# Four query halves of a clustered-attention block keep their softmax in float32, and every step is put into a new order

## The chip, the core and the metric

The kernel runs on one core of a Trainium2 chip. The core has five engines that work side by side and wait for one another by semaphores: TensorE (PE in the profile; its weight loads are the row PEld), VectorE (DVE), ScalarE (ACT), GpSimd (POOL) and SyncE (SP), which issues the DMAs. Each engine works through its own instructions in the order in which the program lists them. The metric is the time of one run in device microseconds.

## The reference

Three blocks follow one another. First comes attention over 16 heads (2 batches of 8 heads, 768 tokens, 64 wide), in which a query sees only those keys that fall to the same one of 16 centroids:

```python
q_assign = argmax(q_n @ c_n.T);  k_assign = argmax(k_n @ c_n.T)
mask   = q_assign[:, None] == k_assign[None, :]
scores = where(mask, 0.125 * q @ k.T, -1e9)
attn   = exp(scores - max(scores)); attn /= sum(attn) + 1e-9
out    = attn @ v                                   # per head: 768 x 768 @ 768 x 64
```

Its output is reshaped to 1536 tokens of 512 and goes through two dense blocks in float32:

```python
h = x @ w_in;   x = elu(h) @ w_out                  # 512 -> 2048 -> 512
y = ((x @ w_a) * (x @ w_b)) @ w_out2                # 512 -> 1536 -> 512
```

## The kernel before

**Tiles.** The 16 heads `g` are worked in 8 pairs `j` (heads 2j and 2j+1). A head's 768 queries are 6 tiles `t` of 128 rows, and three tiles make a half `f`: 0 for t = 0, 1, 2 and 1 for t = 3, 4, 5. So there are 96 query tiles and 16 halves of pairs. Every step is a small function marked `@op`, and the string `ORDER` at the top lists some 2280 steps (`sc:3.1` is the score step of head 3, tile 1). The program runs through that list once, so the list sets the order on every engine, and each step may also name the buffer that it takes (`/sc=0`). No planner is in the program; the list is all there is.

**One query tile.** `sc` (line 692) makes a 128 x 768 tile of scores on PE: four float32r matmuls of 384 columns, since query and key are split into parts that restore the precision, and the cluster mask is a part of the same product. `rm` (L700) finds the row maximum on DVE, into `nm`. `ex` (L713) takes the exponential on ACT, from the scores in PSUM to `pf`, float32 in SBUF, with the row sums beside it. Then the probabilities must be transposed, and this is done in one of two ways.

- *Over PE:* `tr` (L746) transposes half a tile (three 128 x 128 blocks) to PSUM in `tt`; `th` (L750) copies that to float16 on ACT or DVE, the high part; `tl` (L755) subtracts on DVE what `th` has stored from `tt` and writes the rest, the low part, in float16 too.
- *Over DMA:* `hi` (L721) writes a float16 copy of `pf` into `phl`, on ACT or POOL; `lo` (L728) writes the rest there, on POOL or DVE; `td` (L760) has a DMA transpose both into the same place.

In both cases `pt` then holds the transposed probabilities of a half as two float16 parts.

**The product with v.** `av` (L805) makes the product of a half for both heads of a pair, in three pieces (n = 0, 1, 2). V is split as well, into float16 parts `v1` and `v2` (L519, L524), and three of the four combinations are formed: 6 key blocks x 3 combinations x 2 heads = 36 matmuls of 384 columns. The two heads write to the upper and lower 64 partitions of one PSUM tile. `ra`, `rc`, `rx`, `rb` and `re` bring 1 / sum into the layout of that tile (sum + 1e-9 on ACT, reciprocal on DVE, spread on POOL, a transpose on PE, a copy from PSUM), and `ev` (L815) multiplies and stores it into `acc`, over the place in which this pair's V was staged.

**Operands.** `lq`, `lk` and `lp` load a head's queries and a pair's keys, `ka1`, `ka2`, `qa` (L582 on ACT, L584 on POOL), `qb` (L507, DVE), `kb`, `kbd` split them, and `sm`, `m1` to `m5`, `oh`, `ohs`, `ohd` work out the cluster of every query and key of a pair (`sm`, L604, is 12 float32 matmuls of up to 128 columns). `wl`, `wa`, `w0` to `w4`, `wh`, `ws`, `wq` load the float64 weights as integers and make two float32r parts of them on ACT, DVE and POOL. `wm` (L432) is eight bf16 matmuls on zeros that fill PE's idle time at the start. `vr` (L454) looks for the largest V on ACT.

**The dense blocks** `h`, `x2`, `ab`, `o` (L944 to L946) are three float32r matmuls for each product. They begin when the first tokens are through attention.

Of the kernel before, what the change touches and what calls it, by code (L numbers as in the profile page):

```python
# [71 lines left out]
lq:2.0/rawq=0 wm:19 vr:6 tr:0.1.0/tt=2 vr:7 vr:8 wm:22 vr:9 vr:10 vr:11 sc:0.2/sc=0 th:0.1.1.0/pt=0
lq:3.0/rawq=1 tl:0.1.1 vr:12 ka1:2.2 ka1:3.2 vr:13 vr:14 vr:15 th:0.1.0.0 ka2:2.2 lp:1.0/rawp=1 wh:0
mo:0 wm:25 wl:1 rm:0.2/nm=2 sb:0 ws:0 sc:1.0/sc=1 wm:33 wm:34 wm:35 lk:2.0/rawk=0 wq:0 th:0.0.0.0
rm:1.0/nm=3 tl:0.1.0 ex:0.2/pf=2 vtp:0/tt=1 wm:36 wm:37 sc:1.1/sc=0 vtd:0 tl:0.0.0 vbp:0/tt=2 wm:38
hi:0.2.1/phl=0 vbd:0 vs:2 ex:1.0/pf=1 rm:1.1/nm=0 wa:1 tr:1.0.0/tt=1 tr:1.0.1/tt=0 qa:2.1
ex:1.1/pf=1 sc:1.2/sc=1 qa:3.1 w0:1 sm:1/tt=2 lo:0.2.0 sc:0.3/sc=0 wm:39 wm:40 hi:1.1.1/phl=1 w1:1
qb:2.0 w2:1 td:0.2 rm:1.2/nm=1 rm:0.3/nm=2 lo:1.1.2 vs:3 th:1.0.1.1/pt=1 m1:1/mx=1 tl:1.0.1
th:1.0.0.1 vs:0 m2:1 ex:1.2/pf=2 sc:0.5/sc=1 rm:0.5/nm=3 ex:0.3/pf=1/sum=1 hi:1.2.1/phl=2 wh:1 vs:1
tl:1.0.0 sc:0.4/sc=0 rm:0.4/nm=0 tr:0.0.1/tt=0 wm:41 wm:42 wm:43 v1:0.1/v1=0 v1:2.1/v1=1 td:1.1  # L80
lp:2.0/rawp=0 th:0.0.1.1 lo:1.2.2 ex:0.5/pf=0 kbd:2 w3:1 sc:1.3/sc=1 hi:0.5.1/phl=3 qb:3.0 w4:1 m3:1
tr:0.3.1/tt=1 wm:44 wm:45 wm:46 lq:4.0/rawq=0 ka1:4.1 lo:0.5.2 th:0.3.1.1/pt=2 ex:0.4/pf=2
v2:0.2/v2=0 rm:1.3/nm=1 m4:1 m5:1/oht=1 wl:2 tl:0.0.1 sc:1.5/sc=0 oh:1/tt=2 tl:0.3.1 v1:1.1/v1=2
tr:0.3.0/tt=0 ra:0.0/rs=0 v2:1.2/v2=1 td:1.2 tr:0.4.1/tt=1 ex:1.3/pf=0 ohs:1/ohs=0 sc:1.4/sc=1
rm:1.5/nm=2 ka2:3.2 th:0.3.0.1 tl:0.3.0 ex:1.5/pf=1 qa:4.1 rc:0.0 th:0.4.1.0 tr:1.3.1/tt=2
tr:0.4.0/tt=0 rm:1.4/nm=3 ohd:1 av:0.0.0 kbd:3 th:0.4.0.1 tl:0.4.1 av:0.0.1 th:1.3.1.1/pt=3
sc:2.0/sc=0 ex:1.4/pf=2 tl:0.4.0 tl:1.3.1 tr:1.3.0/tt=1 ws:1 rx:0.0/rx=0 sc:2.1/sc=1 wq:1
v1:3.1/v1=3 ka2:4.0 hi:1.5.1/phl=0 hi:1.4.1/phl=1 qb:4.0 ra:0.1/rs=1 av:0.0.2 rm:2.0/nm=0 ka1:5.1
th:1.3.0.1 ex:2.0/pf=0/sum=0 sc:2.2/sc=0 lp:6.0/rawp=1 td:0.5 tr:2.0.1/tt=0 rm:2.1/nm=1 lo:1.4.2
tl:1.3.0 kbd:5 wa:2 v2:3.2/v2=2 lo:1.5.0 ex:2.1/pf=2 rb:0.0/tt=2 sc:3.0/sc=1 th:2.0.1.1/pt=0  # L90
re:0.0.1/rb=0 tr:2.1.0/tt=1 lq:5.0/rawq=1 tr:2.1.1/tt=2 td:1.4 rm:2.2/nm=2 rc:0.1 tl:2.0.1 ka2:5.2
ex:2.2/pf=1 th:2.1.1.1 tr:2.0.0/tt=0 w0:2 sc:3.1/sc=0 hi:2.2.1/phl=2 rx:0.1/rx=1 rm:3.0/nm=3
rm:3.1/nm=0 kbd:4 tl:2.1.1 ex:3.0/pf=2 rb:0.1/tt=2 ev:0.0 v2:2.2/v2=3 qa:5.1 lk:3.0/rawk=1
ex:3.1/pf=0 lq:7.0/rawq=0 td:1.5 re:0.1.1/rb=1 sc:2.3/sc=1 hi:3.1.1/phl=3 lo:2.2.2 w1:2 qb:5.0
th:2.1.0.1 sc:3.2/sc=0 w2:2 lo:3.1.2 rm:3.2/nm=1 sm:2/tt=2 wh:2 rm:2.3/nm=2 w3:2 w4:2 lq:8.0/rawq=1
ex:3.2/pf=1 sc:2.4/sc=0 tl:2.1.0 tr:3.0.0/tt=1 ex:2.3/pf=0/sum=1 m1:2/mx=0 ws:2 hi:3.2.1/phl=1
rm:2.4/nm=3 th:2.0.0.1 m2:2 lo:3.2.2 wl:3 sc:2.5/sc=1 th:3.0.0.1/pt=1 av:0.1.0 tl:2.0.0 vs:11 m3:2
rm:2.5/nm=0 tr:3.0.1/tt=0 td:3.1 ka1:6.1 av:0.1.1 ex:2.4/pf=1 m4:2 m5:2/oht=0 th:3.0.1.1 sc:3.3/sc=0
wq:2 hi:2.4.1/phl=0 ex:2.5/pf=2 oh:2/tt=2 tl:3.0.1 wa:3 vs:4 td:2.2 ra:1.0/rs=0 ohs:2/ohs=1
sc:3.4/sc=1 lo:2.4.0 hi:2.5.2/phl=3 rm:3.3/nm=1 ex:3.3/pf=1 tr:2.3.0/tt=0 av:0.1.2 tr:2.3.1/tt=2  # L100
w0:3 td:3.2 th:2.3.0.1/pt=2 rm:3.4/nm=2 sc:3.5/sc=0 tl:3.0.0 tr:3.3.0/tt=1 ev:0.1 ohd:2 ka2:6.2
rc:1.0 av:1.0.0 ex:3.4/pf=0 lo:2.5.2 tl:2.3.0 qa:7.1 rm:3.5/nm=3 th:3.3.0.1/pt=3 rx:1.0/rx=0 ka1:7.1
ex:3.5/pf=2 av:1.0.1 tl:3.3.0 sc:4.0/sc=1 w1:3 hi:3.5.1/phl=2 tr:3.3.1/tt=0 ka2:7.0 qb:7.0
rm:4.0/nm=0 hi:3.4.1/phl=1 sc:4.1/sc=0 av:1.0.2 lo:3.5.2 rb:1.0/tt=1 th:3.3.1.1 vs:8 td:2.4
ra:1.1/rs=1 rc:1.1 td:2.5 rm:4.1/nm=1 ex:4.0/pf=1/sum=0 tl:3.3.1 sc:4.2/sc=1 th:2.3.1.1 vs:5
tr:4.0.0/tt=0 tl:2.3.1 rm:4.2/nm=2 tr:4.0.1/tt=2 th:4.0.0.0/pt=0 ex:4.1/pf=2 re:1.0.1/rb=0
th:4.0.1.1 lp:3.0/rawp=0 rx:1.1/rx=1 ex:4.2/pf=1 sc:5.0/sc=0 lo:3.4.2 rm:5.0/nm=3 tr:4.1.0/tt=1
v1:5.1/v1=0 hi:4.2.2/phl=0 lo:4.2.2 kbd:6 tl:4.0.0 ex:5.0/pf=0 sc:5.1/sc=1 lq:6.0/rawq=0 th:4.1.0.1
rb:1.1/tt=0 tl:4.0.1 rm:5.1/nm=0 v2:5.2/v2=0 re:1.1.1/rb=1 td:3.5 sc:5.2/sc=0 tr:5.0.0/tt=2 qa:6.1
tl:4.1.0 tr:5.0.1/tt=0 td:3.4 ex:5.1/pf=1 rm:5.2/nm=1 lk:4.0/rawk=0 w2:3 hi:5.1.1/phl=3 qb:6.0  # L110
th:5.0.1.1/pt=1 ex:5.2/pf=0 ev:1.0 tl:5.0.1 sm:3/tt=1 lo:5.1.2 sc:4.3/sc=1 sc:4.4/sc=0 m1:3/mx=1
v1:4.1/v1=2 rm:4.3/nm=2 ra:2.0/rs=0 tr:4.1.1/tt=0 m2:3 hi:5.2.1/phl=2 rm:4.4/nm=3 ex:4.3/pf=1/sum=1
th:4.1.1.1 m3:3 rc:2.0 av:1.1.0 ex:4.4/pf=2 m4:3 hi:4.4.1/phl=1 sc:4.5/sc=1 vs:7 rm:4.5/nm=0
m5:3/oht=1 av:1.1.1 qa:8.1 th:5.0.0.0 sc:5.3/sc=0 tl:4.1.1 lo:5.2.2 v2:4.2/v2=1 rx:2.0/rx=0
oh:3/tt=1 rm:5.3/nm=1 av:1.1.2 td:4.2 vs:6 ex:4.5/pf=0 lo:4.4.2 ohs:3/ohs=0 ev:1.1 ex:5.3/pf=2
sc:5.4/sc=1 tr:4.3.1/tt=0 tr:4.3.0/tt=1 ka1:8.2 sc:5.5/sc=0 lq:9.0/rawq=0 th:4.3.1.1/pt=2 tl:5.0.0
lk:5.0/rawk=1 v1:7.1/v1=1 ka2:8.2 td:5.1 rm:5.4/nm=2 tl:4.3.1 hi:4.5.1/phl=0 rm:5.5/nm=3 qa:9.2
td:5.2 tr:5.3.1/tt=2 lp:4.0/rawp=0 w3:3 av:2.0.0 tr:5.3.0/tt=0 ex:5.4/pf=1 av:2.0.1 ohd:3 td:4.4
hi:5.4.1/phl=3 th:5.3.0.1/pt=3 kbd:7 ex:5.5/pf=2 sc:6.0/sc=1 sc:6.1/sc=0 qb:8.0 ra:2.1/rs=1 qb:9.0
lo:5.4.2 tl:5.3.0 rm:6.0/nm=0 td:5.4 rb:2.0/tt=0 th:4.3.0.1 lo:4.5.2 av:2.0.2 tl:4.3.0 rm:6.1/nm=1  # L120
th:5.3.1.1 ex:6.0/pf=1/sum=0 rc:2.1 w4:3 sc:6.2/sc=1 kbd:8 vs:14 hi:5.5.1/phl=2 rm:6.2/nm=2
re:2.0.1/rb=0 ex:6.1/pf=0 tr:6.0.0/tt=1 tr:6.0.1/tt=0 ex:6.2/pf=1 tl:5.3.1 sc:7.0/sc=0
th:6.0.0.0/pt=0 tl:6.0.0 rm:7.0/nm=3 tr:6.1.1/tt=2 sc:7.1/sc=1 td:4.5 hi:6.2.1/phl=1 lo:5.5.2 ev:2.0
ka1:9.1 vs:12 th:6.1.1.1 th:6.0.1.1 sm:4/tt=1 rm:7.1/nm=0 tl:6.0.1 td:5.5 lo:6.2.2 rx:2.1/rx=1
tr:6.1.0/tt=0 ex:7.0/pf=2 ex:7.1/pf=1 v1:6.1/v1=3 tl:6.1.1 vs:9 m1:4/mx=0 td:6.2 sc:7.2/sc=0
th:6.1.0.0 rb:2.1/tt=2 hi:7.1.1/phl=3 rm:7.2/nm=1 m2:4 ka2:9.2 sc:6.3/sc=1 av:2.1.0 re:2.1.1/rb=1
ex:7.2/pf=0 tr:7.0.0/tt=2 tl:6.1.0 sc:6.4/sc=0 hi:7.2.1/phl=0 rm:6.3/nm=2 lo:7.1.2 v2:7.2/v2=2 m3:4
tr:7.0.1/tt=0 av:2.1.1 rm:6.4/nm=3 ra:3.0/rs=0 m4:4 ex:6.3/pf=1/sum=1 th:7.0.1.1/pt=1 v2:6.2/v2=3
sc:6.5/sc=1 rc:3.0 ex:6.4/pf=2 m5:4/oht=0 hi:6.4.1/phl=2 oh:4/tt=1 th:7.0.0.1 lo:7.2.2 tl:7.0.1
sc:7.3/sc=0 av:2.1.2 tr:6.3.1/tt=0 rm:6.5/nm=0 tl:7.0.0 ohs:4/ohs=1 ex:6.5/pf=0 rx:3.0/rx=0 wl:4  # L130
rm:7.3/nm=1 lq:10.0/rawq=1 lq:11.0/rawq=0 lo:6.4.2 ka1:10.2 ev:2.1 ex:7.3/pf=2 tr:6.3.0/tt=2
sc:7.5/sc=1 hi:6.5.1/phl=1 th:6.3.1.0/pt=2 ka2:10.2 td:7.1 qa:10.1 th:6.3.0.0 rm:7.5/nm=2
tr:7.3.0/tt=1 tl:6.3.0 lo:6.5.2 td:7.2 sc:7.4/sc=0 av:3.0.0 ohd:4 tr:7.3.1/tt=2 lp:5.0/rawp=0 td:6.4
rm:7.4/nm=3 tl:6.3.1 ex:7.5/pf=1 ka1:11.1 th:7.3.1.0/pt=3 qa:11.1 sc:8.0/sc=1 ex:7.4/pf=0 th:7.3.0.0
rb:3.0/tt=0 hi:7.4.1/phl=3 kbd:10 rm:8.0/nm=0 ka2:11.2 qb:11.0 av:3.0.1 sc:8.1/sc=0 tl:7.3.0
av:3.0.2 ex:8.0/pf=2/sum=0 hi:7.5.1/phl=0 rm:8.1/nm=1 re:3.0.1/rb=0 lo:7.4.2 sc:8.2/sc=1 qb:10.0
rm:8.2/nm=2 tr:8.0.1/tt=1 tl:7.3.1 tr:8.0.0/tt=0 lo:7.5.2 ex:8.1/pf=0 kbd:9 th:8.0.1.1/pt=0
# [1024 lines left out]
```

## Time and profile before

| | |
|---|---|
| time, median of 3 runs | 798.59 us (796.79 to 798.82) |
| profiled execution | 803.13 us, of which its instructions span 801.3 us |
| mean granted clock of PE | 0.991 of full speed |
| PE busy | 776.8 us (97%), 4250 matmuls |
| DVE busy | 588.1 us (73%) |
| ACT busy | 409.9 us (51%) |
| POOL busy | 362.1 us (45%) |

The shares of the whole span say little here, because two stretches with different limits follow one another: attention, to some 245 us, and the dense blocks behind it. A busy PE is not a PE at its peak: a matmul counts as busy from its start to the end of its latency, so PE also looks busy in a stretch where it issues less than it could. What PE issues is read from how long a chain of equal matmuls takes, not from its busy time.

### The profile page before, as it was taken

How to read it: one execution, taken by the hardware profiler on the slowest of the kernel's cores; microseconds unless marked ns; L12 is line 12 of the kernel's file. 1: busy time of each engine (PE TensorE's matmuls, PEld its weight loads, DVE VectorE, ACT ScalarE, POOL GpSimd, SP SyncE). 2: the span in 40 equal slices, each digit the busy share in tenths (PEclk: the TensorE clock that was granted, in tenths of full speed). 3: DMA queues.
4: the chain of work that ended last, by engine and by line, in shares of the span. 5: the costliest groups of instructions: out<-in, count | busy, mean ns of one | idle time of the engine just before them, and what ended most of it. 6: DMA issues, size and time to landing. Idle time of an engine off the chain costs nothing.

```text
span 801.3 us, 11434 instructions
## 1 busy us (share of the span) xinstructions
PE 776.8 (97%) x4250; PEld 636.6 (79%) x4250; DVE 588.1 (73%) x842; ACT 409.9 (51%) x710; POOL 362.1 (45%) x293
## 2 busy tenths in 40 slices
...
GB/s 301 108 207 192 199 184 205 192 197 136 159 112 57 63 47 106 79 79 105 80 55 104 80 78 28 82 76 53 1 54 75 82 56 51 53 54 1 52 1 105
DMA packets 98007, 79.09 MB, mean 99 GB/s; under 512 B 81248, under 2 KB 81248, under 8 KB 97952
## 3 DMA queue, kind: packets, MB, share of 16 engines
...
q10 hardware_dynamic: 304, 0.79, 0.3%
q8 instruction: 33, 0.54, 0.3%
q14 instruction: 22, 0.18, 0.1%
...
## 4 chain that ended last, share of the span: by engine, by line
PE 81%; ACT 5%; DVE 5%; DMA 3%; issue 2%; POOL 2%; ACTq 0%; POOLq 0%; DVEq 0%
PE ab L944 8%; PE ab L945 8%; PE ab L946 8%; PE h L944 5%; PE h L945 5%; PE h L946 5%; PE x L946 5%; PE x L945 5%; PE x L944 5%; PE sc L692 5%; PE o L944 4%; PE o L945 4%; PE o L946 4%; PE av L805 4%; ACT pf L713 2%
## 5 line engine op out<-in xcount | busy, mean ns | idle before, releaser
L700 DVE TENSOR_REDUCE nm<-sc 128x1 f32<-128x768 f32 x96 | 90.5, 949 | 5.7 <-PE sc L692 4.8
L713 ACT ACTIVATE pf<-sc,nm 128x768 f32<-128x768 f32 x96 | 86.4, 901 | 13.8 <-DVE nm L700 10.2
L728 POOL TENSOR_TENSOR phl<-pf,phl 128x768 f16<-128x768 f32 x47 | 79.4, 1691 | 23.0 <-ACT phl L721 21.1
L1046 ACT COPY t0ab<-ab 128x512 f32<-128x512 f32 x36 | 21.2, 588 | 109.3 <-PE ab L946 109.3
L1051 DVE TENSOR_TENSOR t1ab<-ab,t0ab 128x512 f32<-128x512 f32 x36 | 24.8, 689 | 63.1 <-ACT t0ab L1046 63.0
L692 PE MATMUL sc<-ka,qa 128*128 128x384 f32 x192 | 58.8, 388 | 8.5 <-ACT pf L713 7.7
L875 ACT ACTIVATE wg<-wraw 128x512 f32<-128x512 f32 x68 | 45.0, 667 | 31.5 <-DMA wraw<-in_w_out_dram 15.5
L805 PE MATMUL av<-pt,v 128*64 128x384 f16 x576 | 55.5, 331 | 2.0 <-DMA pt<-phl 2.0
L892 DVE SCALAR_TENSOR_TENSOR wf<-wraw,wg 128x512 int32<-128x512 int32 x68 | 52.1, 766 | 1.9
L692 PE MATMUL sc<-kb,qb 80*128 80x384 f32 x192 | 50.6, 345 | 1.5 <-DVE qb L670 1.5
L905 DVE SCALAR_TENSOR_TENSOR wg<-wraw,wg 128x512 f32<-128x512 uint32 x68 | 50.2, 738 | 1.6
L755 DVE TENSOR_TENSOR pt<-tt,pt 128x384 f16<-128x384 f32 x92 | 48.9, 546 | 0.7 <-ACT pt L750 0.6
L1062 DVE TENSOR_TENSOR gl<-t1ab,gh 128x512 fp32r<-128x512 f32 x36 | 33.9, 942 | 18.7 <-ACT gh L1057 18.5
L746 PE MATMUL tt<-identf,pf 128*128 128x128 f32 x276 | 44.3, 282 | 3.0 <-DVE pt L755 3.0
L805 PEld LDWEIGHTS <-v 128*64 128x64 f16 x576 | 31.3, 110 | 19.4 <-issue 6.6
L880 DVE TENSOR_SCALAR wg<-wg 128x512 f32<-128x512 f32 x68 | 40.3, 593 | 8.6 <-ACT wg L875 8.6
L692 PEld LDWEIGHTS sc<-ka,qa 128*128 128x128 f32 x192 | 29.7, 192 | 21.1 <-ACT pf L713 16.8
L746 PEld LDWEIGHTS tt<-identf,pf 128*128 128x128 f32 x276 | 33.1, 144 | 11.1 <-DVE pt L755 4.6
L885 DVE TENSOR_SCALAR wg<-wg 128x512 int32<-128x512 int32 x68 | 38.9, 572 | 1.8
L1000 DVE SCALAR_TENSOR_TENSOR t1h<-t0h,h 128x1024 f32<-128x1024 f32 x24 | 29.1, 1216 | 13.2 <-ACT t0h L995 13.2
L1102 DVE TENSOR_TENSOR acc<-o,acc 128x1024 f32<-128x1024 f32 (+1 forms) x12 | 14.2, 1180 | 32.3 <-PE o L946 32.3
L692 PEld LDWEIGHTS sc<-kb,qb 80*128 80x128 f32 x192 | 35.8, 193 | 1.8 <-ACT junk L454 1.8
...
## 6 DMA issues: line engine op xcount, KB each, us to landing
...
acc<-in_v_dram SPq DMA_DIRECT2D x4, 768.0 KB, 11.1
...
```

What stands on the lines that cost most here:

```text
L692: nc.tensor.matmul(s[:, j, :HALF], a[:, qs], b[:, j * HALF : (j + 1) * HALF], start=i == 0, stop=i == 1,)
L700: nc.vector.reduce_max(out=nm, in_=st[g][f"sc{t}"][:, :, :HALF], axis=AX.XY, negate=True)
L713: nc.scalar.activation(pf.rearrange("p (a b) -> p a b", a=2), st[g].pop(f"sc{t}")[:, :, :HALF], AF.Exp, bias=st[g].pop(f"nm{t}"), accum_ou ...
L728: (nc.vector, None, nc.gpsimd)[e].tensor_sub(phl[:, S:], st[g].pop(f"pf{t}"), phl[:, :S])
L746: nc.tensor.transpose(tt[:, k * P : (k + 1) * P], pf[:, o : o + P], identf)
L755: nc.vector.tensor_sub(lo, st[g].pop(f"tt{t}{u}"), hi)
L805: nc.tensor.matmul(pairs[j]["av"][x * 64 : (x + 1) * 64].rearrange("p (a q) -> p a q", a=3), st[2 * j + x][("v1", "v2")[vi]][:, kt_, :], s ...
L892: nc.vector.scalar_tensor_tensor(out=f, in0=raws[n][:, :, 1], scalar=-0x40000000, in1=g, op0=ALU.bitwise_and, op1=ALU.bitwise_or,)
L905: nc.vector.scalar_tensor_tensor(out=g, in0=raws.pop(n)[:, :, 0].bitcast(U32), scalar=2.0 ** -52, in1=g, op0=ALU.mult, op1=ALU.mult,)
L944: nc.tensor.matmul(ps, lhi, rhi, start=first, stop=False)
L945: nc.tensor.matmul(ps, lhi, rlo, start=False, stop=False)
L946: nc.tensor.matmul(ps, llo, rhi, start=False, stop=last)
```

## The change

Four of the 16 halves, named in a new set `WHOLE`, are the first halves of the pairs 1, 3, 4 and 6. In them

- `pt` is one float32 tile of the same size in place of two float16 parts;
- all six tiles (three of each head) go over PE, and `th` copies the float32 transpose from PSUM as it is; there is no `tl`, and no `hi`, `lo`, `td`;
- `aw` takes the place of `av`: one float32 matmul for each key block and head, with the staged float32 V from `acc` as its weights: 12 matmuls of 384 columns in place of 36.

The second halves of those four pairs now go over DMA in all six tiles (four of six before). `ra` may run on DVE. `ORDER` is new from its first step to the first dense block; its last 911 steps are the same. By kind the list now has 40 `tl` less (52), 8 `tr` and 8 `th` more, 4 `hi`, `lo` and `td` less (46), 5 `wm` less, and it moves steps between engines: `hi` from ACT (41 to 28) to POOL (9 to 13) and DVE (0 to 5), `lo` from POOL (47 to 38) to DVE (3 to 8), `th` on ACT 71 to 77 and on DVE 21 to 23, `re` on DVE 2 to 6, `qa` from POOL (5 to 1) to ACT (11 to 15), and one or two steps of `ka1`, `ka2`, `v1`, `ra`.

```diff
+WHOLE = {(1, 0), (3, 0), (4, 0), (6, 0)}
...
 ORDER = """
-lk:0.1/rawk=0 lp:0.0/rawp=0 wm:0 wl:0 lq:0.1/rawq=0 c0:0 vl:0 c1:0 cz:0 c2:0 wm:2 wm:26 wm:27 wm:28
...
+lk:0.1/rawk=0 lp:0.0/rawp=0 wm:0 lq:0.1/rawq=0 c0:0 wm:2 wl:0 cs:0 wm:4 c1:0 kb:0 ka1:1.2 wm:26 c2:0
...
     def pt_of(g, f):
         if f"pt{f}" not in st[g]:
-            st[g][f"pt{f}"] = take(ap, "pt", [P, 3, 2 * NT, P], F16, f"pt{f}_{g}", 4)
+            shape, dt = ([P, 3, NT, P], F32) if (g // 2, f) in WHOLE else ([P, 3, 2 * NT, P], F16)
+            st[g][f"pt{f}"] = take(ap, "pt", shape, dt, f"pt{f}_{g}", 4)
         return st[g][f"pt{f}"]
 
     def parts_of(g, t, u):
         f, a = divmod(t, 3)
+        parts = 1 if (g // 2, f) in WHOLE else 2
         return [pt_of(g, f)[:, a, i * NT + 3 * u : i * NT + 3 * (u + 1)].rearrange("p m q -> p (m q)")
-                for i in range(2)]
+                for i in range(parts)]
...
     @op
-    def ra(j, f):
+    def ra(j, f, e):
         s = pairs[j]["rs", f] = take(ap, "rs", [P, 16], F32, f"rs_{j}_{f}", 2)[:, :6]
-        nc.scalar.activation(s, flat(pairs[j]["sum", f]), AF.Identity, bias=eps)
+        if e:
+            nc.scalar.activation(s, flat(pairs[j]["sum", f]), AF.Identity, bias=eps)
+        else:
+            nc.vector.tensor_scalar_add(s, flat(pairs[j]["sum", f]), 1e-9)
...
+    @op
+    def aw(j, f, n):
+        if n == 0:
+            pairs[j]["av"] = take(psumA, "av", [P, HALF], F32, f"av_{j}_{f}")
+        for kt_ in (2 * n, 2 * n + 1):
+            for x in range(2):
+                g = 2 * j + x
+                nc.tensor.matmul(
+                    pairs[j]["av"][x * 64 : (x + 1) * 64].rearrange("p (a q) -> p a q", a=3),
+                    staged(g)[:, kt_ * D : (kt_ + 1) * D], st[g][f"pt{f}"][:, :, kt_, :],
+                    start=kt_ == 0, stop=kt_ == NT - 1,
+                )
```

In the rows below a name ends in its head or pair and a running number (`pt0_6_1716` is `pt`, half 0, head 6), and line numbers are 2 to 20 higher in the changed kernel.

PE at the product of pair 3, half 0, before: the two heads' float16 products alternate, each behind the load of its V part.

```order
L692 MATMUL sc4_7_1954<-kb_7_1626,qb_7_1262 128x384 x2
L805 LDWEIGHTS v1_6_1768
L805 MATMUL av_3_0_1959<-pt0_6_1716,v1_6_1768 64x384
L805 LDWEIGHTS v1_7_1571
L805 MATMUL av_3_0_1959<-pt0_7_1855,v1_7_1571 64x384
L805 LDWEIGHTS v2_6_1857
L805 MATMUL av_3_0_1959<-pt0_6_1716,v2_6_1857 64x384
```

The same place now: a piece is four float32 matmuls, and they stand between the last scores of head 7 and the first of head 8.

```order
L692 MATMUL sc4_7_1881<-kb_7_1243,qb_7_1179 128x384 x2
L824 MATMUL av_3_0_1890<-pt0_6_1625,acc_66 64x384
L824 MATMUL av_3_0_1890<-pt0_7_1726,acc_66 64x384
L824 MATMUL av_3_0_1890<-pt0_6_1625,acc_66 64x384
L824 MATMUL av_3_0_1890<-pt0_7_1726,acc_66 64x384
L692 MATMUL sc0_8_1898<-ka_8_1617,qa_8_1595 128x384 x2
L692 MATMUL sc0_8_1898<-kb_8_1868,qb_8_1642 128x384 x2
```

Twelve matmuls of a piece have become four, and a matmul loads its own float32 weights.

DVE in the first half of pair 4 before: between the maxima (`nm`) stand the subtractions of L755.

```order
L700 TENSOR_REDUCE nm0_9_2087<-sc0_9_2080 128x1
L755 TENSOR_TENSOR pt0_8_2078<-tt01_8_2065,pt0_8_2078 128x384
L755 TENSOR_TENSOR pt0_8_2078<-tt00_8_2070,pt0_8_2078 128x384
L700 TENSOR_REDUCE nm1_9_2113<-sc1_9_2097 128x1
L755 TENSOR_TENSOR pt0_8_2078<-tt10_8_2093,pt0_8_2078 128x384
L750 CAST pt0_9_2130<-tt01_9_2122 128x384
L755 TENSOR_TENSOR pt0_9_2130<-tt01_9_2122,pt0_9_2130 128x384
L700 TENSOR_REDUCE nm2_9_2148<-sc2_9_2117 128x1
```

The same half now: copies of the float32 transposes and other pairs' steps, no subtraction.

```order
L752 COPY pt0_8_1956<-tt01_8_1938 128x384
L700 TENSOR_REDUCE nm2_8_1958<-sc2_8_1947 128x1
L507 SCALAR_TENSOR_TENSOR qb_10_1962<-rawq_10_1783,qa_10_1877 64x768
L700 TENSOR_REDUCE nm0_9_1995<-sc0_9_1976 128x1
L752 COPY pt0_8_1956<-tt11_8_1981 128x384
L700 TENSOR_REDUCE nm1_9_2011<-sc1_9_1989 128x1
L796 COPY rb_3_1_2021<-rbp_3_1_2016 128x384
L752 COPY pt0_8_1956<-tt20_8_2023 128x384
L700 TENSOR_REDUCE nm2_9_2045<-sc2_9_2032 128x1
```

Between two maxima of this half stands one step in place of two or three.

DVE at the start before: the five steps on the first clusters (`mx`, `tp`, `oht`), then the first weight steps.

```order
L564 TENSOR_TENSOR ka_0_171<-rawk_0_111,ka_0_171 64x768
L407 CAST identb_86<-identf_89 128x128
L619 TENSOR_REDUCE mx_0_221<-tp_0_175 128x24
L624 TENSOR_TENSOR tp_0_175<-tp_0_175,mx_0_221 128x384
L629 TENSOR_TENSOR tp_0_175<-tp_0_175,desc_96 128x384
```

The same place now:

```order
L564 TENSOR_TENSOR ka_0_171<-rawk_0_111,ka_0_171 64x768
L898 TENSOR_SCALAR wg0_176<-wg0_176 128x512
L903 TENSOR_SCALAR wg0_176<-wg0_176 128x512
L910 SCALAR_TENSOR_TENSOR wf0_177<-wraw0_136,wg0_176 128x512
L918 TENSOR_SCALAR wg0_176<-wf0_177 128x512
L619 TENSOR_REDUCE mx_0_246<-tp_0_212 128x24
L624 TENSOR_TENSOR tp_0_212<-tp_0_212,mx_0_246 128x384
```

Four of the five steps on the first weight piece have moved ahead of the cluster steps.

## Rows read from the trace of the kernel before

**Rows 1.** Busy time by stretch: start:end, length, each engine's busy us, PEclk, DMA share, GB/s

```profile
15.00:245.00 230.00, 212.85 (x1656) 169.23 (x1657) 217.65 (x343) 206.34 (x425) 174.55 (x142) 0.97 0.83 173
245.00:801.00 556.00, 552.46 (x2462) 456.43 (x2460) 363.32 (x484) 196.58 (x276) 181.16 (x125) 1.00 0.20 63
```

**Rows 2.** Groups of DVE to 308 us: line, shapes, count | busy us, mean ns | idle before

```profile
L755 DVE TENSOR_TENSOR pt<-tt,pt 128x384 f16<-128x384 f32 x92 | 48.9, 546 | 0.7 <-ACT pt L750 0.6
L507 DVE SCALAR_TENSOR_TENSOR qb<-rawq,qa 64x768 fp32r<-64x768 f32 x16 | 20.1, 1255 | 0.2
L750 DVE CAST pt<-tt 128x384 f16<-128x384 f32 x21 | 11.3, 547 | 2.5 <-PE tt L746 2.4
```

**Rows 3.** Groups of ACT and POOL to 308 us

```profile
L721 ACT CAST phl<-pf 128x768 f16<-128x768 f32 x41 | 34.0, 833 | 0.5
L750 ACT CAST pt<-tt 128x384 f16<-128x384 f32 x71 | 32.6, 477 | 3.8 <-PE tt L746 3.5
L582 ACT ACTIVATE qa<-rawq 128x768 fp32r<-128x768 f32 x11 | 9.3, 843 | 0.0
L728 POOL TENSOR_TENSOR phl<-pf,phl 128x768 f16<-128x768 f32 x47 | 79.4, 1691 | 23.0 <-ACT phl L721 21.1 <-POOL ka L564 0.8
```

**Rows 4.** The chain that ended last: start us, us, what

```profile
67.64 3.99 PE tp L604 x24
...
197.98 2.60 PE tp L604 x24
...
201.69 0.71 PE sc L692 x4
...
222.06 1.10 PE av L805 x12
...
225.11 0.99 PE tt L746 x9
```

**Rows 5.** Groups of PE from 15 to 245 us

```profile
L805 PE MATMUL av<-pt,v 128*64 128x384 f16 x540 | 52.4, 331 | 2.0 <-DMA pt<-phl 2.0
...
L746 PE MATMUL tt<-identf,pf 128*128 128x128 f32 x273 | 43.8, 282 | 3.0 <-DVE pt L755 3.0
...
L432 PE MATMUL warm_ps<-warm 128*128 128x128 bf16 x160 | 11.8, 229 | 0.0
```

**Rows 6.** Time line from 134 us; then durations by tile, min/median/max ns

```profile
136.34 1.65 POOL L728 TENSOR_TENSOR phl<-pf,phl 128x768 f16<-128x768 f32 x1 [0.76 <-POOL ka L564]
136.40 2.39 DVE L507 SCALAR_TENSOR_TENSOR qb<-rawq,qa 64x768 fp32r<-64x768 f32 x1
...
L507 DVE SCALAR_TENSOR_TENSOR qb<-rawq,qa x16: 936/951/2393, 13.5 to 199.9; 64x768 fp32r<-64x768 f32 x16
L728 DVE TENSOR_TENSOR phl<-pf,phl x3: 947/953/2586, 34.5 to 77.1; 128x768 f16<-128x768 f32 x3
L880 DVE TENSOR_SCALAR wg<-wg x14: 384/426/2075, 15.3 to 293.3; 128x512 f32<-128x512 f32 x14
```

**Rows 7.** Who waited for whom from 15 to 250 us: total us, times, longest

```profile
ACT pf L713 <- DVE nm L700: 10.2, 16, 1.6
...
DVE nm L700 <- PE sc L692: 4.8, 11, 1.3
...
DVE pt L750 <- PE tt L746: 2.4, 3, 1.1
```

**Rows 8.** Two five-microsecond stretches, columns as in rows 1

```profile
60.00:65.00 5.00, 2.27 (x11) 1.79 (x12) 4.79 (x10) 4.43 (x9) 3.20 (x3) 0.86 1.09 268
65.00:70.00 5.00, 5.00 (x22) 5.00 (x21) 3.66 (x6) 3.50 (x9) 1.67 (x2) 0.50 1.04 160
```

**Rows 9.** Time line of the start, DVE, ACT and PE

```profile
9.32 0.56 DVE L619 TENSOR_REDUCE mx<-tp 128x24 f32<-128x384 f32 x1 [1.87 <-PE tp L604]
...
14.15 0.79 ACT L674 CAST kb<-ot 16x768 fp32r<-16x768 bf16 x1 [3.61 <-PE ot L662]
...
9.12 2.84 PE L432 MATMUL warm_ps<-warm 128*128 128x128 bf16 x48
```

More of the change, by code (lines that the diff above doesn't have):

```diff
@@ L72 @@
[L72 to L137, printed above, removed]
```

356 lines of the change are left out of this document (210 added, 146 removed).

## Prediction

> **What bounds the kernel now.** The busy time by stretch comes first. Behind 245 us PE is busy for 552.46 of 556 us and no other engine for more than 363; from 15 to 245 us DVE has the least room: 217.65 of 230 us, 12.35 idle, before PE (212.85), ACT (206.34) and POOL (174.55) [rows 1]. The last 911 steps, from the first dense blocks on, are unchanged, so a gain must come from the 230 us of attention; what it saves, the dense blocks pass on, since PE works through them without a gap.
>
> PE's busy time there contains latency. The chain shows what it issues: a score tile costs 0.71 us, a piece of the product with v (12 float16 matmuls) 1.10, nine transposes 0.99, the cluster product 2.60 [rows 4]; 48 warming matmuls take 2.84 [rows 9]. That makes 96 x 0.71 = 68.2; 540 / 12 x 1.10 = 49.5; 273 x 0.11 = 30.0; seven of the eight cluster products, 18.2; 160 x 0.059 = 9.4 [rows 4, 5, 9]: 175 us of 230, the small kinds left out. PE has 55 us of room and spends it waiting in the loop scores, maximum, exponential, transpose. The waits agree: ACT waits 10.2 us for DVE's maxima, DVE only 4.8 for scores [rows 7]. DVE is the engine whose work sets the length.
>
> **The change part by part: DVE.** Off DVE go 40 subtractions `tl` of 0.546 us [rows 2], 21.8 us. On it come 2 `th` and 4 `re`, copies of 128x384 from PSUM, 6 x 0.547 = 3.3 [rows 2]; 5 `lo` at the median 0.953 = 4.8 [rows 6]; 5 `hi`, a copy of 128x768 inside SBUF that DVE doesn't do in this trace. Its bounds are 0.43 (the weight step over 512 columns, median 0.426) and 0.95 (`lo` of the same width) [rows 6]; I take the weight step scaled to 768, 0.64, since it too has one tensor operand: 3.2. The single steps (one `ka1` and one `v1` more, two small `ra` more, one `ka2` less) I take as +0.4, each bounded by a median `qb` of 0.951 [rows 6]. The sum is -21.8 + 3.3 + 4.8 + 3.2 + 0.4 = -10.1 us.
>
> Against it stands a wait that the new DVE steps bring. At 136.40 a `qb` takes 2.39 us instead of its median 0.951: POOL had started `lo` 0.06 us before, and the `qb` ends 0.8 us behind POOL's end, about its own length [rows 6]. DVE steps that work within SBUF are thus held while POOL runs some of its steps; `lo` on DVE shows it too (up to 2.586), `tl`, which reads PSUM, has no such tail (mean 0.546, about its copy's 0.547) [rows 2, 6]. Over 16 `qb` the mean is 1.255, so 0.30 of hold each [rows 2]. The net 11 new steps of this kind cost 11 x 0.30 = 3.3 us; the bounds are 0 and 11 x 1.44 = 15.8 (each as the longest `qb`). I take the mean. DVE nets -6.8 us, bounds -11 and +7.
>
> The Trainium skill ("SBUF — State Buffer", "SBUF: two separate sides") says that VectorE, in a two-port mode or with two SBUF inputs, and GpSimd take a shared pair of ports as an exclusive lock for a whole instruction, and the loser waits. The held `qb` agrees, but most of the 16 were not held. By that rule, with POOL busy in 76% of the stretch, a new step would wait half a POOL `lo` in 76% of the cases; that is the first rival below, worked out there.
>
> **ACT, POOL, DMA.** On ACT 13 `hi` go (13 x 0.833 = 10.8), 6 `th` (2.9) and 4 `qa` (3.4) come [rows 3]: -4.5, and some -3 by `re` and the single steps. POOL loses 9 `lo` of 1.691, 15.2 us [rows 3], and 4 `qa`, against 4 `hi` and a `ka2`. DMA has 4 transposes of 50 less. The loop's other engines fall with DVE, so none takes its place; I give this no gain of its own.
>
> **PE.** 24 more transposes cost 24 x 0.11 = 2.6 us [rows 4]. Twelve pieces `av` of 1.10 go: 13.2 [rows 4]. What comes, a float32 matmul of 384 columns with 64 output rows, is not in this trace. The cluster product is float32: its 12 matmuls stand as 24 records, two for each, of at most 128 columns in 0.108 us [rows 4]. Three times that is 0.325 for a record of 384 columns (its weight load may be in it); the lower end is a float32r score matmul, 0.71 / 4 = 0.177 [rows 4]. Whether the two heads' halves of the array run side by side decides more. The float16 ones do: 1.10 / 12 = 0.092 for 384 columns, half of 0.177. A piece has 4 matmuls, 8 records; as each head's two records follow each other on the same half, only the second of one and the first of the next can overlap: 5 lengths, 5 x 0.325 = 1.63, 12 pieces 19.5 us. One after another it is 8 x 0.325 = 2.6, 31.2 us; at the lower end 5 x 0.177 = 0.9, 10.6 us. I take 19.5, since length and overlap are then each from the row nearest in kind: +6.3 on PE (bounds -2.6 and +18.0). With -2.4 for 40 warming matmuls PE goes from 175 to 182 us, still well under DVE. But scores wait behind a piece that is 0.53 us longer. Of the 8.9 us, 0.4 is the part that shows if PE's share of DVE's waits (4.8 + 2.4 [rows 7]) grows with its work, and all of it if every longer piece is waited for; I take 1.6, near the low end, because PE has room.
>
> **Start.** Four weight steps (medians 0.4 to 0.7) now fill the 1.87 us in which DVE waited for the first cluster product [rows 9]; some 3 us of DVE steps that stood between the first maxima are done earlier. ACT gains less: its 3.61 us wait [rows 9] now holds a `qa` and a weight copy, and the 16 passes over V still end at about the same time. I take -0.8, bounds 0 and -3.
>
> **Sum.** -6.8 (DVE) + 1.6 (PE) - 0.8 (start) = -6.0 us: the profiled execution's 803.13 (span 801.3 and 1.8 around it) becomes 797.1. The median of the runs is 4.5 below the profiled one, and the same difference gives 798.6 - 6.0 = 792.6 us.
>
> **Rivals.**
> 1. *No change, through the hold.* If a new DVE step is held for half a POOL `lo` (0.85 us) in 76% of the cases, 11 of them lose 7.1 us, not 3.3. DVE nets -3.0, and the sum is -3.0 + 1.6 - 0.8 = -2.2: 796.4, about the edge of no change. For it: POOL runs three quarters of the stretch [rows 1]. Against it: a mean hold of 0.30 over the `qb` [rows 2], and POOL itself does 15 us less.
> 2. *Slower: the float32 products don't overlap.* Then PE goes to 175 + 18.0 + 2.6 - 2.4 = 193.5 us. In the forecast PE has 224 - 182 = 42 us in which it waits for others; those waits are the loop's latencies and don't shrink when PE gets more to do. 193.5 + 42 = 235.7 against 230: +5.7, 804.3. It decides from the point at which a piece costs over some 2.1 us (about +12 on PE, which eats the 6 us and more). For it: nothing in the trace shows two float32 streams at once. Against it: the float16 halves overlap in all 48 pieces.
> 3. *More than forecast: the slow clock goes.* From 60 to 65 us PE is busy for 2.27 us of 5; in the next five the granted clock is 0.50, the lower of its levels (1.2 GHz), the cluster product takes 3.99 us instead of 2.60, and DVE falls to 3.66 busy [rows 4, 8]. Over the 230 us the clock is 0.97 [rows 1], 3% or 7 us of PE's work. If the new order leaves no such gap, DVE gets back most of what it idles there, some 4 us: -10, 788.6. Against it: longer pieces and fewer warming matmuls may as well open another.
> 4. *The order costs more than the steps save:* holds near the upper bound, say 11 x 1.2 = 13 us: DVE +3, sum +4, 802.6.
>
> **How the numbers follow.** A measurement here can tell 0.3%, 2.4 us, from no change: 796.2 to 801.0. The forecast, with DVE's net between -11 and -3, spans 787.5 to 796.2: 0.54. Rival 3 beyond it 0.08, rival 1 with what else ends within 2.4 us 0.18, rival 2 0.12, rival 4 0.08. Faster is 0.54 + 0.08 = 0.62, the same 0.18, slower 0.20. The range from 786.5 to 802.0 leaves out about 0.05 below and, of the slower cases, about 0.13 above.
>
> **What the profile of the changed kernel would show.** Right: from 15 to about 239 us DVE busy near 211 us, ACT some 8 less, POOL some 19 less; `tl` x52; a float32 piece on PE taking 1.5 to 1.7 us with its eight records; new DVE `hi` at 0.5 to 0.9 us median, means some 0.3 above; the first dense product some 6 us earlier, everything behind it shifted alike. Wrong: pieces of 2.6 us (rival 2); DVE's `hi` and `lo` at means of 1.6 or more (rival 1, then 4); DVE idle rising where `nm` waits for scores; a granted clock under 0.97 over the stretch; or DVE no longer the busiest, ACT's or POOL's waits for DMA buffers in the all-DMA halves setting the pace instead.

## The result and the profile after

The changed kernel takes 790.28 us (median of 4 runs, 790.17 to 791.92) against 798.31 for the one before; the ratio is 0.9907, 95% interval 0.9888 to 0.9926. The forecast was 792.6. Its profiled execution takes 790.29 us (span 788.5).

The execution of before that is shown above was a long one. A second profile of the same kernel (the first experiment) took 797.79 us, close to the median, and is used here for the comparison. Busy time by stretch in that second profile, from the start to its first dense product at 231.96 us (columns as in [rows 1]):

```profile
0.00:15.00 15.00, 12.72 (x127) 12.18 (x128) 6.61 (x17) 6.46 (x10) 6.32 (x27) 1.00 0.90 292
15.00:232.00 217.00, 202.30 (x1627) 161.16 (x1625) 207.00 (x330) 202.13 (x417) 174.72 (x141) 0.98 0.86 180
```

The same for the changed kernel, to its first dense product at 224.73 us:

```profile
0.00:15.00 15.00, 10.68 (x130) 10.44 (x131) 8.11 (x22) 8.69 (x16) 3.52 (x25) 1.00 0.90 289
15.00:224.70 209.70, 201.24 (x1560) 156.29 (x1558) 195.22 (x305) 191.37 (x397) 160.55 (x134) 0.99 0.84 177
224.70:788.50 563.80, 560.18 (x2502) 462.92 (x2500) 371.18 (x497) 203.26 (x287) 182.79 (x126) 1.00 0.20 64
```

The dense blocks begin 7.3 us earlier and last the same (563.8 us; 564.0 before). All of the gain is in attention. There DVE is busy for 203.3 us (8.11 + 195.22) where it was for 213.6: 10.3 less. It is idle for 21.4 us where it was for 18.4: 3.0 more (1.5 less up to 15 us, 4.5 more behind it). -10.3 + 3.0 is the -7.3; this is bookkeeping, which any engine's busy and idle time would allow, and the cause has to come from the experiments. PE is busy for 96% of the stretch (201.24 of 209.7; 93% before).

Groups of DVE, then ACT and POOL, to 300 us, which answer to [rows 2, 3]:

```profile
L757 DVE TENSOR_TENSOR pt<-tt,pt 128x384 f16<-128x384 f32 x52 | 27.5, 542 | 1.5 <-ACT pt L752 1.4
L507 DVE SCALAR_TENSOR_TENSOR qb<-rawq,qa 64x768 fp32r<-64x768 f32 x16 | 17.3, 1085 | 0.0
L728 DVE TENSOR_TENSOR phl<-pf,phl 128x768 f16<-128x768 f32 x8 | 9.1, 1139 | 0.3 <-issue 0.2 <-ACT phl L721 0.2
L752 DVE COPY pt<-tt 128x384 f32<-128x384 f32 x12 | 6.6, 546 | 0.7 <-PE tt L748 0.7
L721 DVE CAST phl<-pf 128x768 f16<-128x768 f32 x5 | 2.9, 589 | 0.2 <-issue 0.2
...
L721 ACT CAST phl<-pf 128x768 f16<-128x768 f32 x28 | 23.4, 835 | 0.3
...
L728 POOL TENSOR_TENSOR phl<-pf,phl 128x768 f16<-128x768 f32 x38 | 65.8, 1733 | 26.7 <-ACT phl L721 13.1 <-issue 8.2 <-DVE rs L770 2.2
```

The counts and durations are those of the working: 40 subtractions less; `hi` on DVE 0.589 (taken: 0.64). What is off is the hold: the 8 `lo` have a mean of 1.139 and a median of 0.953, the 5 `hi` 0.589 and 0.555 (by tile), so the 13 steps are held for 8 x 0.186 + 5 x 0.034 = 1.7 us together, and the mean of `qb` fell to 1.085, from 1.255 in [rows 2] and 1.141 in the second profile of before.

The waits that answer to [rows 7], in the second profile of before, then in the changed kernel:

```profile
ACT pf L713 <- DVE nm L700: 4.7, 11, 1.5
...
DVE nm L700 <- PE sc L692: 4.4, 13, 0.7
```

```profile
DVE nm L700 <- PE sc L692: 8.1, 18, 1.0
...
ACT pf L713 <- DVE nm L700: 6.5, 12, 1.6
```

DVE waits more for PE's scores (8.1 us for 4.4). ACT doesn't wait less for DVE's maxima (6.5 for 4.7): the 10.2 us of [rows 7] belong to the long execution. One stretch of the chain, at the new float32 pieces:

```profile
123.83 0.70 PE sc L692 x4
124.53 1.44 PE av L824 x8
125.97 0.90 PE sc L692 x4
```

A piece takes 1.44 us from its start to the next matmul (estimated: 1.63; float16: 1.10), and its four matmuls are the eight records that were expected.

### The profile page after: what moved, and what is told of

Read it like the earlier page. It is cut to its first block, busy times and chain, and to the rows that moved or that the text cites. A ratio compares the mean times of both kernels' runs of the same rounds, so it can differ in the third digit from the quotient of the medians.

```text
span 788.5 us, 11243 instructions
## 1 busy us (share of the span) xinstructions
PE 772.1 (98%) x4186; PEld 629.6 (80%) x4186; DVE 574.5 (73%) x821; ACT 403.3 (51%) x699; POOL 346.9 (44%) x285
## 4 chain that ended last, share of the span: by engine, by line
PE 85%; DVE 5%; ACT 4%; DMA 3%; issue 2%; SPq 0%; POOL 0%; ACTq 0%; DVEq 0%
PE ab L962 8%; PE ab L964 8%; PE ab L963 8%; PE h L962 6%; PE h L963 6%; PE x L963 6%; PE x L962 6%; PE h L964 6%; PE x L964 6%; PE sc L692 5%; PE o L964 4%; PE o L962 4%; PE o L963 4%; PE av L810 4%; PE tt L748 3%; DMA wraw<-in_w_in_dram 2%
## 5 line engine op out<-in xcount | busy, mean ns | idle before, releaser
L728 POOL TENSOR_TENSOR phl<-pf,phl 128x768 f16<-128x768 f32 x38 | 65.8, 1733 | 26.7 <-ACT phl L721 13.1
L748 PE MATMUL tt<-identf,pf 128*128 128x128 f32 x300 | 46.0, 277 | 0.2 <-ACT ohs L652 0.2
L748 PEld LDWEIGHTS tt<-identf,pf 128*128 128x128 f32 x300 | 35.2, 141 | 8.8 <-issue 4.3
L692 PEld LDWEIGHTS sc<-ka,qa 128*128 128x128 f32 x192 | 29.2, 191 | 15.9 <-ACT pf L713 13.2
L810 PE MATMUL av<-pt,v 128*64 128x384 f16 x432 | 41.0, 329 | 0.6 <-DMA pt<-phl 0.6
L1026 ACT CAST gh<-t1h 128x1024 fp32r<-128x1024 f32 x24 | 25.3, 1052 | 22.8 <-DVE t1h L1018 22.6
L1075 ACT CAST gh<-t1ab 128x512 fp32r<-128x512 f32 x36 | 22.4, 621 | 26.6 <-DVE t1ab L1069 26.6
## 6 DMA issues: line engine op xcount, KB each, us to landing
acc<-in_v_dram SPq DMA_DIRECT2D x4, 768.0 KB, 11.1
```

Source lines behind the costliest of these rows:

```text
L692: nc.tensor.matmul(s[:, j, :HALF], a[:, qs], b[:, j * HALF : (j + 1) * HALF], start=i == 0, stop=i == 1,)
L728: (nc.vector, None, nc.gpsimd)[e].tensor_sub(phl[:, S:], st[g].pop(f"pf{t}"), phl[:, :S])
L748: nc.tensor.transpose(tt[:, k * P : (k + 1) * P], pf[:, o : o + P], identf)
L810: nc.tensor.matmul(pairs[j]["av"][x * 64 : (x + 1) * 64].rearrange("p (a q) -> p a q", a=3), st[2 * j + x][("v1", "v2")[vi]][:, kt_, :], s ...
```

## The experiments

Differences "over the changed kernel" are taken from the medians. The kernel before ran at 796.5 to 797.3 us beside these runs and at 798.31 beside the result, so by the ratios each such difference is 0.3 to 1.8 us larger.

**Before, once more.** No edit.

> The kernel before once more, to see whether the low clock at 60 to 70 us of its profiled execution (803.13 us, 4.8 above the median of 798.3) belongs to the program. If it does: a profile again shows a held DVE step at about 57 us, PE idle for over 2 us of the next five, a granted clock near 0.5 at 65 to 70 us, and a profiled time within 1 us of the runs. If it was an accident of that execution: no stretch near 0.5 there, a span of some 796.5 us and the first dense product at about 232.5 us in place of 237.3.

Median 798.22 us over 10 runs (794.88 to 800.80); ratio to before 1.0016 (0.9998 to 1.0033). The stretch of [rows 8] in this profile:

```profile
60.00:65.00 5.00, 3.40 (x21) 2.83 (x20) 4.55 (x8) 4.98 (x11) 3.04 (x3) 0.96 1.24 218
65.00:70.00 5.00, 5.00 (x30) 4.98 (x30) 4.08 (x7) 4.12 (x9) 3.77 (x3) 0.70 1.05 231
```

Neither expectation was right alone. The dip of PE and the slow clock behind it are there again, so they belong to the program, but smaller (3.40 busy and 0.70, not 2.27 and 0.50). The `lo` on DVE just ahead took 1.07 us here and 2.59 in the execution shown above. A held step of 1.5 us more, a longer gap on PE and a longer slow stretch thus came together once and made that execution some 5 us longer; which of them made how much isn't shown.

**The float32 halves in the order of before.** In the four halves the steps were exchanged one for one and 24 transposes with their copies put between the others, where a PSUM buffer was free and the exponential at least 6 steps back (fewer for some). At pair 3, for example:

```diff
-tl:6.0.0 ... hi:6.2.1/phl=1 ... lo:6.2.2 ... td:6.2 ... av:3.0.0
+tr:6.2.0/tt=1 ... tr:6.2.1/tt=2 th:6.2.0.1 ... th:6.2.1.1 ... aw:3.0.0
```

> The order of before with nothing moved, only the four halves done in float32: 24 subtractions go (24 x 0.546 = 13.1 us of DVE), 12 tiles change from hi, lo and DMA to two transposes and two copies each (PE 24 x 0.33 = +7.9 us, ACT 24 x 0.48 - 11 x 0.83 = +2.4, POOL about -18), and 12 pieces of 1.29 us take the place of 12 of 1.10 (+2.3 on PE). Theory (DVE's work sets the length, whatever the order): 13.1 off DVE, some 2 to 3 us of the PE work shows, 786 to 789 us. Rival (the new order makes the gain; freed DVE time turns into waits for scores and transposes where nothing else has been put): 794 to 799 us. In between, 789 to 794: both.

812.27 us, ratio to before 1.0187 (1.0170 to 1.0203): slower than either theory. From the start to the first dense product at 244.6 us:

```profile
0.00:15.00 15.00, 11.63 (x134) 10.88 (x135) 7.08 (x17) 6.95 (x11) 6.06 (x26) 1.00 0.89 287
15.00:244.60 229.60, 212.38 (x1642) 164.70 (x1642) 194.14 (x305) 204.45 (x430) 151.22 (x127) 0.99 0.70 150
```

DVE did lose 12.4 us of work (201.2 for 213.6), and its idle time rose by 25.0 (43.4 for 18.4). Where it went, in DVE's waits and then the time line at 200 us (PE, DVE, ACT):

```profile
DVE nm L702 <- PE sc L694: 17.5, 25, 2.4
DVE mx L621 <- PE tp L606: 8.6, 3, 3.9
```

```profile
200.65 0.88 PE L750 MATMUL tt<-identf,pf 128*128 128x128 f32 x6 [0.95 <-ACT pt L754]
202.51 0.49 PE L606 MATMUL tp<-cblk,rawp 128*128 128x128 f32 x2 [0.98 <-ACT pt L754]
...
205.41 0.56 DVE L621 TENSOR_REDUCE mx<-tp 128x24 f32<-128x384 f32 x1 [3.92 <-PE tp L606]
...
206.52 0.48 ACT L798 COPY rb<-rbp 128x384 f32<-128x384 f32 x1 [3.69 <-PE rbp L793]
```

PE stands twice for a copy on ACT that must free a PSUM buffer, then works through the 2.7 us of the cluster product, and DVE and ACT both wait some 3.8 us behind it: no score stands ahead of the product for them to work on.

**The same, placed later.** The same steps; the added transposes 10 to 14 steps behind the exponentials.

> As the run with the float32 halves in the order of before (812.3 us), but the 24 added transposes stand 10 to 14 steps behind their exponential in place of 6 or fewer, and their copies up to 9 steps behind the transposes: another placement of the same steps. If the order of before cannot take the new steps wherever they are put between others: 806 to 816 us. If the 14 us lost were bad luck of one placement: under 800 us.

818.06 us, ratio to before 1.0266 (1.0236 to 1.0295), 2 us above the slower of the two expected ranges. Two placements by a simple rule lose some 15 and 21 us. This shows that the parts gain nothing when they are merely put in, not that no placement in the old order would do.

**The subtractions put back.**

```diff
+    spare = const.tile([P, HALF], F16, name="spare")
+    def ts(g, t, u):
+        nc.vector.tensor_sub(spare, st[g][f"tt{t}{u}"], parts_of(g, t, u)[0])
```

> The changed kernel with a subtraction on DVE (128x384, from PSUM, written to a tile that nobody reads) behind each of the 48 copies of the float32 halves: 48 x 0.546 = 26.2 us of DVE work of the kind that the change removed, and nothing else. Theory (DVE's work sets the length of attention): +18 to +26 us, 808 to 816 us. Rival (the loop's waits set it, DVE's work hides in its idle time): +3 to +10, 793 to 800 us.

817.84 us, ratio to before 1.0257 (1.0239 to 1.0275): 27.6 us over the changed kernel. To the first dense product at 251.4 us:

```profile
0.00:15.00 15.00, 11.90 (x139) 11.50 (x140) 8.73 (x22) 9.28 (x18) 3.93 (x26) 1.00 0.89 292
15.00:251.40 236.40, 209.29 (x1551) 157.90 (x1549) 220.24 (x352) 192.49 (x395) 162.33 (x134) 0.98 0.73 157
```

DVE's busy time is 25.6 us longer (229.0 for 203.3), its idle time 1.0 (22.4 for 21.4). The work that was added to DVE shows in full, and the time lies above even the theory's range. Not all of it need be DVE's time: an added subtraction also keeps a PSUM buffer until it is done, and the weight loads of PE's transposes wait 10.6 us for these steps. That DVE's idle time hardly rose speaks for the work; the two weren't separated.

The run doesn't show what the new order is worth alone. It puts back 25.6 us of DVE work where the change saved 10.3, so that DVE has 229.0 us of it, and 213.6 before. Scaled to 10.3 us, the cost would be 11.1 us and the time some 801 us, about that of before (798.3); this is an estimate, and no run has the new order with all halves in float16.

**DVE relieved.** The 5 `hi` go to ACT and the 8 `lo` to POOL:

```diff
-... lo:6.3.0 ... hi:6.4.0/phl=1
+... lo:6.3.2 ... hi:6.4.1/phl=1
```

> The changed kernel, with the 13 steps of hi and lo that it has on DVE given back: 5 hi to ACT (+5 x 0.835 = 4.2 us there), 8 lo to POOL (+8 x 1.73 = 13.9). DVE loses 2.9 + 9.1 = 12.0 us. Theory (DVE's work sets the length, and a step less on it is worth its time): 779 to 786 us. Rival (the steps stand on DVE because POOL's queue would bring the DMA transposes too late): DVE waits instead, 788 to 800 us.

792.77 us (ratio to before 0.9953, 0.9931 to 0.9974), 2.5 over the changed kernel and within the rival's range. To the first dense product at 227.0 us, and DVE's largest wait:

```profile
0.00:15.00 15.00, 11.04 (x129) 10.74 (x130) 8.05 (x21) 8.62 (x15) 3.52 (x25) 1.00 0.89 286
15.00:227.00 212.00, 203.99 (x1563) 157.68 (x1560) 187.54 (x292) 194.30 (x402) 173.35 (x142) 0.98 0.83 175
```

```profile
DVE nm L700 <- PE sc L692: 17.0, 26, 1.7
```

DVE is busy for 7.7 us less and idle for 10.0 more, most of it waiting for scores (17.0 us, 8.1 in the changed kernel). The rival was right that DVE waits instead, but its reason isn't borne out: PE's products wait for DMA transposes a little in the changed kernel (1.1 us on their weight loads) and not at all here. What the trace shows is ACT waiting 2.5 us for POOL's `lo` to give back `pf`, where it was 0.4. DVE work that is moved to ACT and POOL thus gains nothing; what it would be worth if it were simply gone isn't shown.

**Four matmuls listed head by head.**

```diff
-        for kt_ in (2 * n, 2 * n + 1):
-            for x in range(2):
+        for x in range(2):
+            for kt_ in (2 * n, 2 * n + 1):
```

> The changed kernel, with the four float32 matmuls of a piece listed head by head (A, A, B, B) and not alternating. Alternating, the changed kernel's trace shows both heads' records starting within 0.01 us of each other every 0.32 us, 1.29 us a piece. Theory: listed head by head only the middle records overlap, 7 or 8 steps of 0.32 us, 2.3 to 2.6 a piece, 12 to 15.5 us more on PE; of that 18% shows, as the prediction took for PE work, +2 to +3: 792.5 to 793.5 us. Rival (PE has no room left, most of it shows): +8 to +15, 798 to 806 us. If the list order doesn't matter to the overlap: pieces of 1.29 us and 790.3 us.

790.64 us, ratio to before 0.9926 (0.9910 to 0.9942): no change, as the third expectation had it. A piece:

```profile
124.54 1.52 PE L824 MATMUL av<-pt,acc 128*64 128x384 f32 x8
125.99 0.62 PE L692 MATMUL sc<-ka,qa 128*128 128x384 f32 x2
```

1.45 us again. This alone leaves two readings: no overlap in either kernel, or an overlap that doesn't need neighbours in the list.

**Heads over the pieces.** The first piece holds four matmuls of one head, the last four of the other:

```diff
-        for kt_ in (2 * n, 2 * n + 1):
-            for x in range(2):
+        for x, kt_ in [(x, k) for x in range(2) for k in range(NT)][4 * n : 4 * n + 4]:
```

> The changed kernel, but the 12 float32 matmuls of a half go head by head over the three pieces: all four of the first piece on one head, two and two in the second, all four of the third on the other. Four matmuls on one half of the array have no partner there, so if the two heads overlap in the changed kernel the first and third piece take 8 x 0.32 = 2.6 us and the second 1.29: +2.6 us of PE per half, +10.3 in all. Theory (PE has room, 18% shows): +1.9, about 792.2 us. Rival (PE has none left after the new order): +6 to +10, 796 to 800 us. If the pieces stay at 1.29, the two records that start together belong to one matmul, and heads don't overlap at all: 790.3 us.

The chain of this kernel at the same place:

```profile
125.85 2.72 PE av L823 x8
128.57 0.90 PE sc L692 x4
...
130.51 1.45 PE av L823 x8
```

2.72 us without a partner, 1.45 with one, which is close to half: the heads do overlap, almost in full, and with the run before it the second reading holds. The Trainium skill ("TensorEngine Tiling (Array Packing)", "Key Properties") says that tiles operate independently and can load weights and multiply in parallel; the trace agrees for float32 in 64 columns (2.72 against 1.45).

The time is 798.88 us, ratio to before 1.0023 (1.0007 to 1.0039), 8.6 over the changed kernel for 8 x 1.28 = 10.2 us more on PE. 84% of it shows (some 70 to 110% by the intervals of the two ratios), and DVE's wait for scores goes from 8.1 to 15.2 us. The rival was right.

**The same on before.** The float16 products of five first halves, head by head over the pieces:

```diff
+        both = [(p, x) for p in prods for x in range(2)]
+        if f == 0 and j in (1, 3, 4, 5, 6):
+            both = [(p, x) for x in range(2) for p in prods]
```

> The kernel before, with the float16 products of the first halves of the pairs 1, 3, 4, 5, 6 listed head by head over the three pieces, as in the run on the changed kernel that cost 8.6 us for about 9.2 us of PE. Without a partner 12 float16 matmuls of 384 columns should take some 2.1 us in place of 1.10 (0.177 each, a quarter of a score tile): two pieces in each of five halves, about +10 us of PE. It tests the prediction's share of 18% on the kernel that it was taken from. Theory (before has PE room, the new order used it up): +1 to +4 us, 798 to 801 us. Rival (PE work shows as fully before): +7 to +10, 804 to 807 us.

802.46 us, ratio to before 1.0086 (1.0057 to 1.0114), some 6.9 us. A piece without a partner:

```profile
136.97 2.14 PE L808 MATMUL av<-pt,v 128*64 128x384 f16 x12
139.04 0.62 PE L692 MATMUL sc<-ka,qa 128*128 128x384 f32 x2
```

It takes 2.07 us, 0.97 more, in two pieces of each half; the mixed ones are up to 0.35 longer: 10 x 0.97 + 5 x 0.35 = 11.4 us at most. About 60% shows (40 to 80% by the interval), between the two expectations. The two shares, 60 and 84%, aren't clearly apart; both are well above 18%.

**More warming.** Six more `wm` behind the first cluster product.

> The changed kernel with six more warming steps (48 matmuls) on PE between the first cluster product and the first one-hot transposes, where its trace has PE idle for 2.91 us before 14.5 us and a granted clock of 0.66 from 15 to 20 us. Theory (idle PE brings the slow clock, and the first scores are late by it): the clock from 15 to 20 us is 1.0, the first three score tiles take 0.71 in place of 1.0 to 1.6 us, and the end comes 0.4 to 1.2 us earlier: 789.1 to 789.9 us. Rival (DVE sets the pace there too): the clock is back, but the time is 790.3 within 0.3.

Two stretches of the changed kernel, then of this one:

```profile
10.00:15.00 5.00, 2.09 (x38) 2.00 (x36) 4.69 (x11) 4.08 (x10) 1.26 (x1) 1.00 1.04 330
15.00:20.00 5.00, 5.00 (x41) 4.09 (x39) 4.26 (x6) 4.81 (x13) 4.76 (x4) 0.66 1.04 350
```

```profile
10.00:15.00 5.00, 5.00 (x92) 4.89 (x90) 4.69 (x11) 4.08 (x10) 1.27 (x1) 1.00 1.04 336
15.00:20.00 5.00, 4.61 (x53) 3.51 (x50) 4.84 (x7) 4.81 (x13) 4.75 (x4) 1.00 1.06 353
```

The clock is back, and the time is 791.25 us (ratio to before 0.9942, 0.9923 to 0.9961): no gain, and a little above both expected ranges. The first maximum starts 0.61 us earlier, but DVE then waits 0.62 us for a score at 22.5 us and is where it was.

**Two more halves in float32.** The first halves of pairs 2 and 5, put in by the same rule.

> The changed kernel with two more first halves, of the pairs 2 and 5, in float32, their steps put in between the others where a buffer of PSUM is free: 12 subtractions less (6.5 us of DVE), 12 transposes' worth of 0.33 us and six pieces 0.34 us longer (+6.0 on PE). Theory (DVE and PE are both near their limit now): no gain, 790 to 797 us. Rival (DVE's work alone counts): 784 to 787 us.

799.05 us, ratio to before 1.0034 (1.0018 to 1.0050): 8.8 us lost, more than either range allowed. DVE is busy for 3.7 us less than in the changed kernel and waits 19.8 us for scores. No kernel of these runs beats the changed one.

## Why the prediction was right

**The step that carries it is borne out in part.** That DVE's work counts is shown one way: 25.6 us more of it cost 27.6 us. The other way it isn't: of the four runs that took DVE work away from the kernel that they started from (by 12.4, 10.3, 7.7 and 3.7 us) and gave other engines more, none was faster. Two pieces of the prediction's evidence were weaker than it took them for: ACT's wait of 10.2 us for the maxima was that of one long execution (4.7 in the second profile), and the 55 us of room on PE are taken up below.

DVE's busy time fell by 10.3 us, close to the 10.1 of the uncontended working, and that is partly luck. Added up step by step, the durations of DVE's steps fell by 13.2 us (221.5 for 234.7): 10.6 of work and 2.6 of holds. But the records of neighbouring steps overlap by some 0.08 us, which a count of durations such as 40 x 0.546 leaves out, so the busy time fell by less.

**The hold was mis-sized, with the wrong sign.** 3.3 us were added for new steps that POOL holds. Measured are 1.7 us on them, while the old steps were held some 4.3 us less: the 16 `qb` took 17.4 us in place of 18.2, and 18 short weight steps (`wg`) in attention 9.1 in place of 12.5. The mean of 0.30 came from where the old order had put the steps, and the order changed. What decides is seen at 125 us of the changed kernel, POOL, then DVE:

```profile
125.11 1.28 POOL L942 TENSOR_TENSOR wf<-wf,w0h 128x512 f32<-128x512 f32 x1
...
125.44 1.77 DVE L728 TENSOR_TENSOR phl<-pf,phl 128x768 f16<-128x768 f32 x1
```

The `lo` starts within the POOL step and ends 0.82 us behind its end. Counted over the twelve profiles: of 192 `qb` on DVE, 104 started while POOL was idle, and none of these took more than 0.96 us, also where a POOL step began during it (34). Of the 88 that started within a POOL step 52 are longer than 1.0 us, up to 2.45, and 51 of these end 0.81 us behind the end of that POOL step. The 764 subtractions `tl` of these profiles, which read PSUM, never exceed 0.56, though 620 of them start within a POOL step. The Trainium skill's rule of the exclusive lock ("SBUF — State Buffer", "SBUF: two separate sides") says just this: who starts first has the ports for its whole instruction. The prediction weighed it by POOL's share of busy time, 76%, and by a mean; what it needed was where in the list the steps stand.

**PE's term was too small, for the wrong reason.** Its size was put too high: 12 x (1.44 - 1.10) = 4.1, not 6.3, since the heads overlap almost in full; with the transposes and the warming steps 4.1 + 2.6 - 2.4 = 4.3 us. But the share that shows isn't 18%: it is about 60% in the old order and 84% in the new. That makes 2.6 to 3.6 where 1.6 was taken, an estimate from runs that made pieces longer in other places. Behind 15 us DVE's idle time rose by 4.5, most of it (3.7) waits of `nm` for scores, which the prediction had named as a sign of being wrong. "PE has 55 us of room" was the faulty step: PE's idle time lies in the loop's waits and can't be filled at will, as these two shares show. Rival 2's own arithmetic (those waits don't shrink) was nearer.

**The start** was put at -0.8; up to 15 us DVE's idle time fell by 1.5.

**So two errors cancelled:** DVE 3.5 us better, idle time 2.2 worse than the terms for PE and the start (+0.8), -7.3 for -6.0.

**What was missing was the order.** The prediction priced the parts and gave the order only -0.8 at the start. Steps exchanged in the old order: 812 and 818 us. New order with the float32 halves: 790. So the float32 halves lost in the old order, in the two placements that were run, and gain in the new one; what the order gives without them isn't shown. The traces of the slower runs suggest why: in the four runs named above DVE waits 17.0 to 19.8 us for scores (8.1 in the changed kernel), so that work taken off DVE is worth its time only if PE's queue has the next scores ahead of it.

**The rivals.** The hold by POOL (1) and the cost of the order (4) did not come about; the float32 products do overlap (2 fell). The slow clock (3): at 60 to 70 us it is gone in the changed kernel:

```profile
60.00:65.00 5.00, 5.00 (x43) 4.16 (x42) 4.90 (x8) 5.00 (x12) 3.08 (x4) 1.00 0.42 106
65.00:70.00 5.00, 5.00 (x48) 3.94 (x50) 4.83 (x9) 4.59 (x9) 4.76 (x5) 1.00 0.69 190
```

A new slow stretch at 15 to 20 us costs nothing that can be measured. How much of the gain is the clock's isn't settled. An upper bound for the second profile of before: PE's clock was granted at 0.66 from 40 to 45 us, at 0.96 and 0.70 in the two stretches from 60 to 70 us, and at 1.00 else, so PE lost 5 x (0.34 + 0.04 + 0.30) = 3.4 us at most (an estimate).
